# A fused attention and feed-forward kernel: AV and the second feed-forward on two 64-row halves from the third batch on

## The chip, the cores and the metric

One Trainium2 chip; the program runs on 1 of its cores. The metric is device time in microseconds, the median of the runs. The core's engines are TensorE (PE in the profile, and PEld for its weight loads), VectorE (DVE), ScalarE (ACT), GpSimd (POOL) and SyncE (SP, which here only issues DMAs). Matmuls write to PSUM, which has eight banks of 512 f32 a partition.

## The reference, cut to what matters

Attention with 16 query heads on 4 key/value heads over 8 batches of 384 positions, then a feed-forward with a squared relu over all 3072 rows:

```python
k = np.repeat(k, group, axis=1); v = np.repeat(v, group, axis=1)    # group = 4
scores = (1 / np.sqrt(64)) * np.matmul(q, k.transpose(0, 1, 3, 2))
attn = np.exp(scores - np.max(scores, axis=-1, keepdims=True))
attn = attn / (np.sum(attn, axis=-1, keepdims=True) + 1e-09)
attn_out = np.matmul(attn, v)                         # (8, 16, 384, 64)
x = attn_out.transpose(0, 2, 1, 3).reshape(3072, 1024)
h = np.maximum(x @ w_in, 0.0)                         # w_in 1024 x 2048
out = h * h @ w_out                                   # w_out 2048 x 1024
```

Inputs and output are f32; the kernel computes in bf16 with f32 sums. It leaves out the subtraction of the maximum, and gets the sum of a softmax row from a column of ones that is appended to v.

## The kernel before, in words

**A recorder with a clock.** The kernel is not written as loops for each engine. A class `Recorder` takes operations one by one (`R.add`, line 45): the engine, a function that issues the instructions, the tiles read and written, and a cost in us. It derives what each operation must wait for, keeps an estimated clock for each engine, and at the end `emit` (line 86) writes each engine's instructions in the order of recording, with semaphore waits. The operations are chosen by the loop at line 694: at each step it lists the candidates (scores `sc`, AV `av` and `av2`, a piece of the feed-forward `ffn`, some transposes) with the time at which each could start by the estimated clocks, and takes the one of best rank among those that are ready. `R.when` gives such a time; `used` and `pick` (line 200) choose a PSUM bank.

**The work of one batch.** A batch has 384 rows, three tiles of 128.

- Scores (`burst_small`, matmuls at line 362): kT times qT for each head. The head size is 64, so a matmul uses 64 of the 128 rows of the array, and two run side by side, one on rows 0 to 63 and one on rows 64 to 127, in two banks. ACT takes both banks at once through exp into `expT` (line 372).
- AV (`av`, matmuls at line 388): eight chunks a batch, each 18 matmuls with all 128 rows: the stationary operand is a 128 x 128 block of expT, the moving one 65 columns of `v_aug`. A chunk goes to one bank, in two parts of nine; between the two the loop can't put anything else (`av2` is ranked 2 and always ready). DVE then takes the reciprocal of the sums (line 397) and multiplies (line 403) into `o_sb`; after each second chunk SP transposes two chunks by DMA into `xT` (line 408).
- The first feed-forward: 16 tiles of 128 columns of w_in, each a sum over 8 blocks of 128 rows. In most batches this runs as quads of four tiles on 64-row halves (`quad`, matmuls at line 483): a pair of half matmuls works on two tiles at a time, in two banks, and a second phase swaps the halves, so that each bank gets both halves of the sum. The second phase waits for the first (`after`), since two halves must not write one bank at the same time; the phases of two pairs take turns. The banks are 4 to 7. A quad's eight pieces have eight half matmuls of 384 columns each. DVE takes the relu (line 496) and most of the squares (line 503), ACT a few squares (line 500), into `h2T`. Scores of the next batch are put between these pieces (`split` is true in this stretch). The last batch and part of the first use `up_part` instead (line 446), with 128 rows.
- The second feed-forward (`downs`, `down_part`, matmuls at line 545): for each of two column halves and three row tiles, 16 matmuls of 128 rows x 512 columns in four parts of four, alternating between banks 6 and 7. DVE copies the bank to `y_sb` (line 554) and SP stores it (line 557).

**The order.** In the steady state, the loop for feed-forward batch b first records the quads of b with the scores of b + 1 between their pieces, then seven AV chunks of b + 1, one part of the second feed-forward, the last AV chunk, and the rest of the second feed-forward of b. So scores and quads use 64-row halves, AV and the second feed-forward all 128 rows. SP's queue then holds four xT transposes, the kT and qT transposes for a later batch, and the six output stores. POOL's queue holds the loads of q, k and v, which wait for those transposes, and a copy into v_aug (line 275).

Of the kernel before, what the change touches and what calls it, by code (L numbers as in the profile page):

```python
# [5 lines left out]
ALU = mybir.AluOpType  # L6
# [135 lines left out]
def bass_gqa_attention__then__ffn_squared_relu_kernel(  # L142
# [12 lines left out]
    HKV = 4  # L155
# [249 lines left out]

    def turn_o_dma(b, g):
        o = (b * HKV + g) % NO
        R.add("sync", lambda e: e.dma_start_transpose(
            out=xT[b % NXT][:, 2 * g:2 * g + 2, :].rearrange("p c (i t) -> p (c i) t", i=NJ),
            in_=o_sb[o].ap().rearrange("p s f d -> p (s f d)")),  # L410
            reads=[("o_sb", o, 0), ("o_sb", o, 1)], writes=[("xT", b % NXT, 2 * g), ("xT", b % NXT, 2 * g + 1)],
            dma=f"turn_o{o}", cost=0.9, shared=(7.0, 1.1))
# [99 lines left out]
    def up_tile(b, c):  # L512
        at = []
        return [up_part(b, c, at, k0, k0 + 4) for k0 in (0, 4)]

    def downs(b):

        items = []
        for jj in range(2 if b == 0 else 0):
            ats = [[] for _ in range(NJ)]  # L520
            for tiles in ((0, 1), (2,)):
                for half in range(2):
                    for i3 in tiles:
                        for part in (2 * half, 2 * half + 1):
                            items.append(down_part(b, jj, i3, 512 * jj, 512 * jj + 512, part, ats[i3]))
        for jj in range(2 if b else 0):
            for i3 in range(NJ):
                last = b == B - 1 and (jj, i3) == (1, NJ - 1)
                for c0, c1 in ((512, 896), (896, 1024)) if last else ((512 * jj, 512 * jj + 512),):
                    at = []  # L530
                    for part in range(4):
                        items.append(down_part(b, jj, i3, c0, c1, part, at))
        return items

    def down_part(b, jj, i3, c0, c1, part, at):
        n = c1 - c0

        def piece():
# [11 lines left out]
            if part == 3:  # L550
                yb = y_n[0] % (2 * NY)
                y_n[0] += 1
                ysl = y_sb[yb // 2][:, (yb % 2) * 512:(yb % 2) * 512 + n]
                R.add("vector", lambda e: e.tensor_copy(ysl, bank(i)[:, 0:n]),  # L554
                      reads=[("bank", i)], writes=[("y", yb)], cost=0.08 + n / 960)
                rows = out[b * S:(b + 1) * S, :].rearrange("(p j) f -> j p f", j=NJ)[i3]
                put = lambda: R.add("sync", lambda e: e.dma_start(rows[:, c0:c1], ysl),
                                    reads=[("y", yb)], writes=[("out", b, i3, c0)], dma=f"y{yb}", cost=0.6)
                stored.append(("out", b, i3, c0))
                if b:  # L560
                    put()
                else:
                    held_back.append(put)

        need = [("w_out", jj, part // 2)] + [("h2T", c) for c in range(4 * part, 4 * part + 4)]
        return 0, need, (6, 7) if part == 0 else None, piece

# [62 lines left out]
    LOW, MID, HIGH = tuple(range(6)), (4, 5), (6, 7)  # L630
    smalls = []
# [60 lines left out]
    av_open = None  # L692
    margin = 0.5
    while av_q or av_open or sc_q or o_q or lanes or ff["now"] or ff["tiles"] or ff["down"]:
# [35 lines left out]
        if av_open is not None:  # L730
            cand.append((now, 2, "av2"))
        elif av_q:
            b, c = av_q[0]
            needs = {(b, c // 2 * NJ + j, 3 * (c % 2) + t) for j in range(NJ) for t in range(3)}
            if needs <= scored and ff["b"] >= b - NXT + (not ff["tiles"]):
                cand.append((max(R.when(reads=av_reads(b, c)), open_bank(spare)) + wait, 2, "av"))
        if o_q:
            cand.append((max(R.when(reads=o_q[0][2]), open_bank(spare)) + wait, 3, "o"))
        at_edge = not ff["now"] and not lanes and av_open is None
        if sc_q:  # L740
# [4 lines left out]
            ok = ok and pairs // 2 * NJ + NEX > b * NU + max(x for _, x, _ in tiles)  # L745
            if b and not split:
                ok = ok and at_edge and (u > 0 or pairs >= 8 * b and ff["b"] == b - 1 and len(ff["tiles"]) >= 4)
# [19 lines left out]
        if f_head is not None:  # L767
            chunks, need, banks, piece = f_head
            if x_done[ff["b"]] >= chunks:
                t = R.when(reads=need)  # L770
                if banks:
                    t = max(t, max(open_bank([i]) for i in banks) if split or opening else open_bank(banks))
                cand.append((t, 5, "ffn"))
        if split and at_edge and len(ff["tiles"]) < 4 and not (sc_q and sc_q[0][1]):
            split = False
            R.clock["tensor"] += 0.1
            continue
        if split:
            inside = [x for x in cand if x[2] in ("sc", "ffn")]
# [7 lines left out]
        ready = [x for x in cand if x[0] <= now + (0.0 if split else 0.05)]  # L787
        what = min(ready, key=lambda x: x[1]) if ready else min(cand)
# [3 lines left out]
        if split and what[2] not in ("sc", "ffn"):  # L792
            split = False
# [9 lines left out]
        elif what[2] == "av":  # L803
            b, c = av_q.pop(0)
            av_open = (b, c, av(b, c, spare))
            next(av_open[2])
        elif what[2] == "av2":
            b, c, rest = av_open
            av_open = None
# [11 lines left out]
        elif what[2] == "sc":  # L821
            b, u = sc_q.pop(0)
            if b and not split:
                split = True
                R.clock["tensor"] += 0.1
# [5 lines left out]
        else:  # L831
            if opening:
                split = True
                R.clock["tensor"] += 0.1
# [31 lines left out]
```

## Time and profile before

| what | value |
|---|---|
| median of 3 runs | 418.99 us (418.98 to 420.0) |
| profiled execution, its span | 417.1 us; its own time is not listed apart, so the runs' median stands beside it, 1.9 us longer |
| granted TensorE clock | 1.000 |
| PE matmuls / weight loads | 4322 / 4322 |
| L545, second feed-forward | 168.2 us busy, x784 |
| L483, quads | 160.0 us busy, x1728 halves |
| L362, scores | 53.9 us busy, x384 halves |
| L388, AV | 39.0 us busy, x1152 |
| L397 and L403, DVE after AV | 186 and 557 ns each, x64 |
| L496 and L503, relu and square on DVE | 552 and 568 ns each |
| L554, copy of the result on DVE | 691 ns for 512 columns |

The span is the time from the first to the last instruction of the program on the core; the runs' time is a little longer, since it has the launch's edges too. "Busy" counts the time in which at least one instruction of a group runs. Matmuls overlap: a matmul of 384 columns shows 323 ns of its own, but the next can start long before it ends, so the pace is read from the starts. The chain of work that ended last is followed back from the last instruction to what released it; its rows in order of time give the start, the time to the next row, the engine and line, and the number of instructions. A timeline row gives the start, the length, the engine and line, the shapes (rows*columns of the array, then the moving operand) and how many instructions were merged. Times are from the start of the span. In PEld rows a bracket gives idle time of the loading unit and what the profile thinks ended it.

### The profile page before, as it was taken

How to read it: one execution, taken by the hardware profiler on the slowest of the kernel's cores; microseconds unless marked ns; L12 is line 12 of the kernel's file. 1: busy time of each engine (PE TensorE's matmuls, PEld its weight loads, DVE VectorE, ACT ScalarE, POOL GpSimd, SP SyncE). 2: the span in 40 equal slices, each digit the busy share in tenths (PEclk: the TensorE clock that was granted, in tenths of full speed). 3: DMA queues.
4: the chain of work that ended last, by engine and by line, in shares of the span. 5: the costliest groups of instructions: out<-in, count | busy, mean ns of one | idle time of the engine just before them, and what ended most of it. 6: DMA issues, size and time to landing. Idle time of an engine off the chain costs nothing.

```text
span 417.1 us, 9610 instructions
## 1 busy us (share of the span) xinstructions
PE 413.2 (99%) x4322; PEld 235.2 (56%) x4322; DVE 202.1 (48%) x438; ACT 158.7 (38%) x180; POOL 47.4 (11%) x62
## 2 busy tenths in 40 slices
PE   8999999999999999999999999999999999999997
PEld 6565754557445564455645565455744557446544
DVE  3765751487314682156712666135842458324312
ACT  6958510386018510384005830069000970004300
POOL 8580000323003000200030000000000000000000
PEclk9999999999999999999999999999999999999999
DMA  9999999999989029900599006710052001420012
GB/s 181 188 190 194 206 186 176 234 182 128 191 152 160 7 52 194 203 10 2 75 214 168 2 2 108 184 52 2 3 126 77 27 2 21 127 78 5 0 75 77
DMA packets 96921, 44.40 MB, mean 106 GB/s; under 512 B 77296, under 2 KB 90864, under 8 KB 96880
## 3 DMA queue, kind: packets, MB, share of 16 engines
q0 software_dynamic: 36544, 17.44, 32.7%
q1 hardware_dynamic: 59664, 25.86, 28.4%
q8 instruction: 34, 0.56, 0.6%
q10 hardware_dynamic: 672, 0.49, 0.4%
q14 instruction: 7, 0.06, 0.0%
HBM read 35.65 MB, written 12.58 MB: 116 GB/s over the span
## 4 chain that ended last, share of the span: by engine, by line
PE 97%; ACT 2%; DVE 0%; issue 0%
PE ps L545 40%; PE ps L483 34%; PE ps L388 8%; PE ps L362 8%; PE ps L446 6%; ACT expT L372 2%; PE ps L608 1%; PE ps L421 0%; PE ps L336 0%; PE ps L316 0%; PE ps L299 0%; DVE y_sb L554 0%
## 5 line engine op out<-in xcount | busy, mean ns | idle before, releaser
L372 ACT ACTIVATE expT<-ps 128x1024 bf16<-128x1024 f32 (+1 forms) x145 | 135.9, 1033 | 132.6 <-PE ps L362 132.6
L545 PE MATMUL ps<-w_out_sb,h2T 128*128 128x512 bf16 (+2 forms) x784 | 168.2, 375 | 0.0
L483 PE MATMUL ps<-xT,w_in_sb 64*128 64x384 bf16 x1728 | 160.0, 323 | 0.0
L545 PEld LDWEIGHTS ps<-w_out_sb,h2T 128*128 128x128 bf16 x784 | 75.1, 98 | 86.6
L483 PEld LDWEIGHTS ps<-xT,w_in_sb 64*128 64x128 bf16 x1728 | 83.0, 94 | 57.8 <-DVE hr L496 2.5
L496 DVE TENSOR_SCALAR hr<-ps 128x384 f32<-128x384 f32 x108 | 55.2, 552 | 76.8 <-PE ps L483 76.8
L554 DVE COPY y_sb<-ps 128x512 f32<-128x512 f32 (+2 forms) x49 | 33.3, 680 | 112.1 <-PE ps L545 112.1
L362 PE MATMUL ps<-qT,kT 64*128 64x256 bf16 (+2 forms) x384 | 53.9, 324 | 0.7 <-ACT expT L372 0.6
L503 DVE TENSOR_TENSOR h2T<-hr 128x384 bf16<-128x384 f32 x102 | 51.8, 568 | 0.0
L388 PEld LDWEIGHTS ps<-v_aug,expT 128*128 128x128 bf16 x1152 | 36.9, 97 | 5.5 <-ACT h2T L500 1.3
L388 PE MATMUL ps<-v_aug,expT 128*128 128x65 bf16 x1152 | 39.0, 193 | 0.0
L403 DVE TENSOR_TENSOR o_sb<-ps,rinv 128x384 bf16<-128x384 f32 x64 | 35.7, 557 | 2.2
L446 PE MATMUL ps<-xT,w_in_sb 128*128 128x384 bf16 x160 | 27.5, 326 | 0.0
L456 ACT ACTIVATE h2T<-hr 128x384 bf16<-128x384 f32 x20 | 10.3, 523 | 44.1 <-DVE hr L454 44.1
L362 PEld LDWEIGHTS ps<-qT,kT 64*128 64x128 bf16 x384 | 17.7, 94 | 15.8 <-issue 1.7
L275 POOL COPY v_aug<-v_st 128x768 bf16<-128x768 bf16 x8 | 7.0, 874 | 153.7 <-PE ps L388 91.1
L500 ACT ACTIVATE h2T<-hr 128x384 bf16<-128x384 f32 x6 | 3.1, 522 | 50.0 <-DVE hr L496 50.0
L446 PEld LDWEIGHTS ps<-xT,w_in_sb 128*128 128x128 bf16 x160 | 15.4, 98 | 10.0 <-issue 0.2
L454 DVE TENSOR_SCALAR hr<-ps 128x384 f32<-128x384 f32 x20 | 10.9, 556 | 11.8 <-PE ps L446 11.7
L241 POOL DMA_DIRECT2D q_st<-in_q_dram x17 | 14.9, 887 | 1.0 <-POOLq L851 0.8
L397 DVE RECIPROCAL rinv<-ps 128x6 f32<-128x6 f32 x64 | 11.9, 186 | 2.4 <-PE ps L388 2.4
L209 POOL DMA_DIRECT2D k_st<-in_k_dram x7 | 5.3, 756 | 48.4 <-DMA qT<-q_st 48.4
(32 smaller groups left out, 63.3 us busy)
## 6 DMA issues: line engine op xcount, KB each, us to landing
out_dram<-y_sb SPq DMA_DIRECT2D x47, 256.0 KB, 2.7
q_st<-in_q_dram POOLq DMA_DIRECT2D x14, 384.0 KB, 8.0
w_in_sb<-in_moe_w_in_dram POOLq DMA_DIRECT2D x8, 512.0 KB, 15.2
w_out_sb<-in_moe_w_out_dram POOLq DMA_DIRECT2D x4, 1024.0 KB, 29.2
v_st<-in_v_dram POOLq DMA_DIRECT2D x8, 192.0 KB, 10.0
k_st<-in_k_dram POOLq DMA_DIRECT2D x7, 192.0 KB, 5.3
q_st<-in_q_dram POOLq DMA_DIRECT2D x3, 192.0 KB, 5.2
xT<-o_sb SPq DMA_TRANSPOSE x28, 2.8
```

The lines of the kernel that those rows point to most:

```text
L241: i = R.add("gpsimd", lambda g: g.dma_start(q_st[st][:, h0:h1, :], q[b, h0:h1].rearrange("h (p j) d -> p h (j d)", j=NJ)), writes=[("q_st" ...
L362: mm = pe.matmul(ps[:, base + x, m * wide:(m + 1) * wide], kT[b % 2][64 * x:64 * x + 64, u, :], q_cols(b, u // NJ, x, c0, c0 + wide))
L372: R.add("scalar", lambda e: e.activation(dst, src, AF.Exp, scale=0.125), reads=keys, writes=[("expT", (b * NU + u) % NEX, t) for u, _, _ i ...
L388: m = pe.matmul(po[:, f - 6 * s2, 0:D + 1], w, v_aug[b % 2][:, g * NJ + j, 0:D + 1], start=(j == 0), stop=(j == NJ - 1))
L397: R.add("vector", lambda e: e.reciprocal(rinv[r].ap().unsqueeze(2), po[:, :, D:D + 1]), reads=[("bank", i)], writes=[("rinv", r)], cost=0.22)
L403: R.add("vector", lambda e: e.tensor_tensor(dst, srcv, rbv, ALU.mult), reads=[("bank", i), ("rinv", r)], writes=[("o_sb", o, s2)], cost=0.48)
L446: m = pe.matmul(bank(i)[:, 0:S], w_in_sb[:, kc, c * 128:(c + 1) * 128], xT[b % NXT][:, kc, :], start=(kc == 0), stop=(kc == NKC - 1))
L483: m = pe.matmul(bank(4 + xs[x])[:, 0:S], w_in_sb[r, kc, c * 128:(c + 1) * 128], xT[b % NXT][r, kc, :], start=(phase < 2 and kc == 0), stop ...
L496: R.add("vector", lambda e, r=r, i=i: e.tensor_scalar_max(hr[r][:, :], bank(4 + i)[:, 0:S], 0.0), reads=[("bank", 4 + i)], writes=[("hr", ...
L503: hr_read[r] = (R.add("vector", lambda e, c=c, r=r: e.tensor_tensor(h2T[:, c, :], hr[r][:, :], hr[r][:, :], ALU.mult), reads=[("hr", r)], ...
L545: m = pe.matmul(bank(i)[:, 0:n], h2T[:, c, i3 * 128:(i3 + 1) * 128], w_out_sb[:, c, c0:c1], start=(c == 0), stop=(c == NFC - 1))
L554: R.add("vector", lambda e: e.tensor_copy(ysl, bank(i)[:, 0:n]), reads=[("bank", i)], writes=[("y", yb)], cost=0.08 + n / 960)
```

## The change

For feed-forward batches 2 to 6 (`on_halves`), and AV of batches 3 to 7 that is recorded with them:

- AV runs on halves (`av_halves`). A chunk owns a pair of banks, (0, 1) or (2, 3) in turn. Its first part has nine pairs of half matmuls, each 64 rows x 65 columns: rows 0 to 63 go to the first bank and rows 64 to 127 to the second. The second part swaps the halves, and waits for the end of the first part's last matmul. DVE's reciprocal and multiplication read both banks at once, three blocks from each.
- Parts of AV are kept apart: `since` counts the pieces of feed-forward since the last AV part, and an AV part is taken only after one such piece, or after two among the quads. AV may begin among the last quads, once the scores of the next batch are all recorded.
- The second feed-forward runs on halves (`down_pair`): three pairs of tiles, in banks (4, 5), (6, 7) and (2, 3), each in two phases of four pieces of eight half matmuls x 512 columns; the second phase swaps the halves and waits for the first. The pieces of the pairs take turns. The copies of a pair's two banks and its two stores are recorded together, after its last piece.
- The tiles of the first feed-forward in the last batch may use banks 0 to 3 in place of 6 and 7.
- The recorder's estimate for entering or leaving the stretch of quads, 0.1 us, is 0 where both sides are on halves.

```diff
+    def on_halves(b):
+        return 2 <= b < B - 1
+
+    def av_halves(b, c, pairs):
+
+        g, s2 = c // 2, c % 2
+        p = pick_pair(pairs)
+        held.update(p)
+
+        def mm(pe, y):
+            for n in range(NJ):
+                for j in range(NJ):
+                    for x in range(2):
+                        f, h = 6 * s2 + NJ * x + n, (x + y) % 2
+                        r = slice(64 * h, 64 * h + 64)
+                        w = expT[r, (b * NU + g * NJ + j) % NEX, f % 2, (f // 2) * 128:(f // 2) * 128 + 128]
+                        m = pe.matmul(ps[:, p[x], n * DP:n * DP + D + 1], w, v_aug[b % 2][r, g * NJ + j, 0:D + 1],
+                                      start=(n + j + y == 0), stop=(n + j + y == 2 * NJ - 1))
+            return m
+
+        keys = [("bank", i) for i in p]
+        lead = R.add("tensor", lambda pe: mm(pe, 0), reads=av_reads(b, c), writes=keys, cost=0.285)
+        yield lead
+        held.difference_update(p)
+        R.add("tensor", lambda pe: mm(pe, 1), reads=av_reads(b, c), writes=keys, cost=0.285, after=(lead,))
...
@@ downs
+        if on_halves(b):
+            t = [(jj, i3) for jj in range(2) for i3 in range(NJ)]
+            p, q, r = [down_pair(b, t[2 * n:2 * n + 2], (4, 6, 2)[n]) for n in range(3)]
+            items = p[0:4] + q[0:2] + p[4:8] + q[2:4]
+            for n in range(4):
+                items += [r[n], q[4 + n]]
+            items += r[4:8]
-        for jj in range(2 if b else 0):
+        for jj in range(2 if b and not on_halves(b) else 0):
...
+    def down_pair(b, tiles, base):
...
+                def mm(pe):
+                    for c in range(4 * k, 4 * k + 4):
+                        for h in range(2):
+                            x, r = (y + h) % 2, slice(64 * h, 64 * h + 64)
+                            jj, i3 = tiles[x]
+                            m = pe.matmul(bank(base + x)[:, 0:512], h2T[r, c, i3 * 128:(i3 + 1) * 128],
+                                          w_out_sb[r, c, jj * 512:(jj + 1) * 512],
+                                          start=(y + c == 0), stop=(y == 1 and c == NFC - 1))
+                    return m
+
+                ends.append(R.add("tensor", mm, reads=need, writes=[("bank", base + x) for x in range(2)],
+                                  cost=4 * (512 / 2400 + 0.0025), after=(ends[3],) if y == 1 and k == 0 else ()))
+                if len(ends) == 8:
+                    held.difference_update((base, base + 1))
+                    for x, (jj, i3) in enumerate(tiles):
+                        store(b, i3, 512 * jj, 512 * jj + 512, base + x)
...
@@ the loop that chooses
+    since, AMONG = 9, 2
...
+            late = on_halves(ff["b"]) and not (sc_q and sc_q[0][0] == ff["b"] + 1)
+            inside = [x for x in cand if x[2] in ("sc", "ffn") or late and (x[2] == "av2" or x[2] == "av" and since >= AMONG)]
...
+        if since < (AMONG if split else 1) and on_halves(ff["b"]):
+            ready = [x for x in ready if x[2] not in ("av", "av2")] or [] if split else ([x for x in ready if x[2] not in ("av", "av2")] or ready)
...
+        since = 0 if what[2] in ("av", "av2") else since + (what[2] == "ffn")
```

In the instructions as recorded, a batch's loop now reads: scores and quads as before; in the last two quads an AV part after every second piece, four in all, and a fifth after the last; then eleven AV parts, each behind one piece of the second feed-forward; then the remaining 13 pieces of it with no AV between. `store` holds what `down_part` did for the copy and the store. On SP the order is three xT transposes, two stores, the fourth xT transpose, the kT and qT transposes, and the other four stores. TensorE has 5522 matmuls and as many weight loads in place of 4322.

## The prediction

> **What bounds the kernel now.** I read the page's busy shares first, then its chain of work that ended last:
>
> ```profile
> PE 413.2 (99%) x4322; PEld 235.2 (56%) x4322; DVE 202.1 (48%) x438; ACT 158.7 (38%) x180; POOL 47.4 (11%) x62
> PE 97%; ACT 2%; DVE 0%; issue 0%
> ```
>
> TensorE is never long without a matmul, and 97% of the chain is TensorE's own; the 2% of ACT lies in the first 13 us. So neither a transfer nor another engine holds the middle of the run, and the question is only at what pace the matmuls follow each other. The chain in order of time shows it for the end of one batch's loop and the start of the next (start us, us, what):
>
> ```profile
> 297.94 3.94 PE ps L388 x126
> 301.89 0.86 PE ps L545 x4
> 302.75 0.55 PE ps L388 x18
> 303.30 19.86 PE ps L545 x92
> 323.15 0.54 PE ps L362 x4
> 323.69 1.30 PE ps L483 x16
> ```
>
> Paces from it: the second feed-forward (L545) 19.86 / 92 = 0.216 us a matmul of 128 rows x 512 columns; the first on halves (L483) 1.30 / 16 = 0.081 us a half, so 0.1625 us a pair of 64-row halves x 384 columns; AV (L388) 0.55 / 18 = 0.0304 us a matmul of 128 x 65. The step from 384 to 512 columns is 0.0533 us for 128 columns, 0.416 ns a column, and leaves 2.5 ns a matmul over: a pair of halves costs the same as one full matmul of that width. 65 columns would be 29.6 ns by the same line. So everything runs at the column rate, and what is left over is small. The chain has it at two places: 126 AV matmuls at 0.0304 are 3.83, and 3.94 stand there; four score halves (L362, two pairs of 512) should be 0.43, and 0.54 stand there. Both are where TensorE goes from 64-row halves to 128 rows or back. The timeline puts a number on it (start us, us, engine and line; three windows):
>
> ```profile
> 322.13 1.03 PE L545 MATMUL ps<-w_out_sb,h2T 128*128 128x512 bf16 x4
> 323.09 0.60 PE L362 MATMUL ps<-qT,kT 64*128 64x512 bf16 x4
> ...
> 372.14 1.03 PE L545 MATMUL ps<-w_out_sb,h2T 128*128 128x512 bf16 x4
> 373.01 0.49 PE L446 MATMUL ps<-xT,w_in_sb 128*128 128x384 bf16 x2
> ...
> 347.15 0.81 PE L483 MATMUL ps<-xT,w_in_sb 64*128 64x384 bf16 x8
> 347.89 0.20 PE L388 MATMUL ps<-v_aug,expT 128*128 128x65 bf16 x1
> ```
>
> Four L545 matmuls are due 4 x 0.216 = 0.863 after their first starts. At 372.14 the next operation also has 128 rows, and it starts 0.87 later: on time. At 322.13 the next is on halves, and it starts 0.96 later. At 347.15 four pairs are due 0.65 later, at 347.80; AV starts at 347.89. The single records give 95 to 97 ns at all nine such places between 147.6 and 347.7 us. **One change of row mode costs 0.096 us**; I know of no other idle time in these batches.
>
> **The change, part by part.** *Removed:* the loop of feed-forward batch 2 starts at 122.7 us on halves in both kernels. From there to the end of batch 6 the old one changes mode nine times (AV of batches 3 to 7 begins at 147.6, 197.6, 247.6, 297.6 and 347.6; scores and quads resume at 172.7, 222.7, 272.8 and 322.8). The new one stays on halves, and changes once at the end, to L446, where the old one did not (373.01 above). Eight fewer: 8 x 0.096 = **-0.77 us**.
>
> *Second feed-forward on halves:* 5 batches x 96 matmuls become 480 pairs of 64 x 512. Score pairs of that shape stand in the old trace at the column rate (two in 0.43, as at 80.33 us in the chain), and L483 pairs show the same; so 0.216 a pair, no change. Three pairs of tiles each own two banks (4 and 5, 6 and 7, 2 and 3) and their turn-round is interleaved: a second phase, which adds to banks that the other half wrote, waits for the end of the first phase's fourth piece, with at least two pieces, 1.7 us, between. The last pair leaves two copies to VectorE at once. L554 copies take 0.69 us and, like the relus (0.55 long, 0.475 apart), should start some 0.08 less apart, 0.61 (an estimate); the second ends about 0.39 + 0.61 + 0.69 = 1.7 us after the last matmul starts (0.39 is that matmul's own length), and the scores that want banks 2 and 3 stand one matmul, one score pair and two quad pieces behind it, 0.216 + 0.216 + 1.30 = 1.73 us. That just fits; 0 to 0.05 us a batch, at most +0.25, and I take 0.
>
> *AV on halves:* 5 x 8 x 18 = 720 full matmuls become 720 pairs of 64 x 65, in parts of nine pairs. The old trace has no pair narrower than 256 columns, so this price is bounded. From below: the column rate, 29.6 ns a pair against 30.4 now: 720 x 0.8 = -0.6 us. From above: each half costs a full matmul's 30.4, so 60.8 a pair: +21.9 us. I take 30.4, no change, by the weight loads and the order of issue:
>
> ```profile
> 347.31 0.26 PEld L483 LDWEIGHTS ps<-xT,w_in_sb 64*128 64x128 bf16 x4
> 347.89 0.39 PEld L388 LDWEIGHTS ps<-v_aug,expT 128*128 128x128 bf16 x11 [0.32 <-ACT h2T L500]
> ```
>
> Four half loads are over 0.26 us after the first began, which is one pair's 0.1625 and one load of 0.094 (its mean in the groups by shape): two halves load side by side. Eleven full loads follow each other by 0.029. In the single records the second half starts 3 ns behind the first, matmul and load alike, four instructions in 5 ns. The sequencer's own waits (records that no view lists) show how far it runs ahead: it passed the wait for AV's v_aug at 346.03 us, 20 matmuls before AV's first at 347.89, and at 97.3 us it passed eight instructions within 48 ns of a semaphore. A part's 18 halves therefore stand ready when the wide piece ahead of it (0.65 us among quads, 0.86 in the second feed-forward) ends.
>
> A rule of the Trainium skill speaks against this: "TensorE: Matmul & The Clock Gate", section "Wait — 56ns, not 53.3ns?", says that starts of matmuls never come closer than about 25 ns, however narrow they are. By it a pair is 50 ns, and the sum would be 720 x 19.6 = +14.1 us, not 0; the 3 ns between two halves in this trace say that the rule does not hold between row halves, though none here is that narrow.
>
> *What moves with AV:* the old order is seven AV chunks (126 matmuls) in a block, then one more; the new one spreads 16 parts over the last quads and the first half of the second feed-forward. Each chunk's reciprocal (0.186) and multiplication (0.557) move with it. DVE is the engine to look at: after the last quad ends it owes two relus and three squares at 0.475 and 0.467 apart, 0.95 + 1.4, and a start of 0.2, 2.6 us, before the fourth piece of the second feed-forward, which reads the last four h2T tiles. Ahead of that piece stand three pieces of 0.863 and four AV parts of 0.274: 3.7 us. Cover of 1.1 us; one more chunk's 0.74 in front still fits. AV's second part waits for its first part's end with a whole piece between. Of TensorE's queue, all that follows waits behind such a wait, so these are the places where it would hurt. On SP the fourth xT transpose now stands behind two output stores, some 6 us later than before, and lands about 7 us ahead of the next batch's quads; kT and qT transposes behind it and the POOL loads that wait for qT serve a batch later. None of it is on the path.
>
> **Sum.** -0.77 + 0 + 0 + 0 = -0.77 us. The profiled span is 417.1 us, the median of the runs 418.99; the 1.9 us around the span are not touched. 418.99 - 0.77 = **418.2 us**, -0.18%.
>
> **Rivals.** A measurement of this kernel can tell about 0.3%, 1.26 us, from no change.
>
> *AV loses its last nanosecond too.* Old AV loses 0.8 ns a matmul against the column rate, with a 35 ns step after about every four of 29. If pairs drop that, -0.77 - 0.6 = -1.4 us, 417.6 us, just over the 0.3%. For it: nothing in wide pairs shows such a step. Against: the load of 128 columns is the same.
>
> *The narrow pairs are paced by instructions, not columns: slower.* Place: the 80 AV parts. Twice the instructions in the same 0.55 us a chunk; the mechanism decides from 30.4 + 0.77 / 720 = 31.5 ns a pair, where the gain is gone, and from 30.4 + (0.77 + 1.26) / 720 = 33.2 ns the change is slower by over 0.3%. Price if halves wait in turn: +21.9 - 0.8, 440.1 us; if a pair takes 35 ns, 720 x 4.6 - 0.77 = +2.5, 421.5 us. For it: no pair under 256 columns in the trace. Against: the 3 ns and the run-ahead.
>
> *A wait takes the place of the mode change.* The two places above with covers of 1.1 us (h2T) and about nothing (banks 2 and 3). If each batch stood 0.5 us, +2.5 - 0.77 = +1.7, 420.7 us. Against: only DVE work not seen in the old order could do it.
>
> *The 0.096 us is not the mode's and stays:* 419.0 us. Against: it appears at each change and is missing at L545 to L446 and L545 to L388.
>
> **Chances.** Forecast 0.45; AV's nanosecond gone 0.20; pairs of 33 to 45 ns 0.13; pairs of 45 to 61 ns 0.12; a wait 0.06; no effect 0.04. Faster by over 0.3%: 0.20. Within: 0.45 + 0.04 = 0.49. Slower: 0.13 + 0.12 + 0.06 = 0.31. The range goes from the second case less a tenth or two, 417.4, to the 35 ns pair, 421.5; outside are the 0.12 and the upper half of the 0.13.
>
> **What would show it.** Timeline at L545's successor: a quad or score on time, no 0.096. Chain: the batch period, 50.01 us now (the rows at 273.14 and 323.15), at 49.8. A part of 18 AV halves in 0.27 us; 0.54 means the instruction rival. Eight down halves in 0.86. Waits: TensorE behind DVE at the first scores or at the fourth down piece means the third rival. The forecast is wrong if a narrow pair takes over 33 ns.

## The result, and the profile after

| | median us | runs | |
|---|---|---|---|
| before | 419.08 | 12 (418.95 to 420.06) | |
| after | 418.24 | 12 (418.0 to 418.7) | ratio 0.9978, 95% interval 0.997 to 0.9987 |

The change saves 0.84 us, by the interval 0.5 to 1.3 us. The profiled execution of after took 418.54 us, its span 416.7 us at a granted clock of 1.000. The page's busy shares and its chain for the kernel after:

```profile
PE 413.1 (99%) x5522; PEld 236.3 (57%) x5522; DVE 202.9 (49%) x438; ACT 159.3 (38%) x180; POOL 46.8 (11%) x62
PE 97%; ACT 1%; DVE 1%; issue 0%
```

1200 more matmuls, and TensorE is as busy and as long in the chain as it was: a share of busy time can't show this change. It has to be read from starts. The chain of after in order of time (start us, us, what): the first quads of a batch, then from the first piece of its second feed-forward to the next batch:

```profile
223.39 1.30 PE ps L524 x16
...
249.29 0.86 PE ps L635 x8
250.43 0.86 PE ps L635 x8
251.57 0.86 PE ps L635 x8
...
261.80 11.22 PE ps L635 x104
273.24 1.30 PE ps L524 x16
```

Eight halves of 512 columns take 0.86, four pairs at 0.2158. Between two of them lies an AV part: 250.43 - 249.29 - 0.86 = 0.28 us for nine pairs of 65 columns. The 104 halves then run through to 273.02, and one pair of scores (L362, 0.21, too short for this list) leads to 273.24, where the next quads start. The chain's row for the same place a batch earlier starts at 223.39: a batch takes 49.85 us, where it took 50.01.

The timeline of TensorE shows the joints (start us, us, line and shape; three windows of after):

```profile
272.64 0.38 PE L635 MATMUL ps<-w_out_sb,h2T 64*128 64x512 bf16 x2
272.86 0.38 PE L362 MATMUL ps<-qT,kT 64*128 64x512 bf16 x2
273.07 1.46 PE L524 MATMUL ps<-xT,w_in_sb 64*128 64x384 bf16 x16
274.41 0.61 PE L362 MATMUL ps<-qT,kT 64*128 64x512 bf16 x6
...
370.81 1.89 PE L635 MATMUL ps<-w_out_sb,h2T 64*128 64x512 bf16 x16
372.63 0.66 PE L487 MATMUL ps<-xT,w_in_sb 128*128 128x384 bf16 x3
```

One pair of 512 columns from 272.64 leads to the scores at 272.86 and these to the quads at 273.07, each 0.216 later: the 0.096 us at the old scores is gone. The eight pairs from 273.07 are due 1.30 later, at 274.37, and the second scores start at 274.41, some 0.04 late (0.036 by the single records). At the end eight pairs from 370.81 are due 1.73 later, at 372.54; L487 with 128 rows starts at 372.63, late by the one change of mode that is left.

I went through all starts of the single records and took off what each matmul costs at the column rate (columns / 2.4 + 2.5 ns). From 123 to 373 us only six places of more than 25 ns remain in after: changes of mode at 123.04 and 372.32 (96 ns each), and the 0.036 us at 174.5, 224.4, 274.2 and 324.1. Between those two changes lie 249.28 us; in before the same stretch has 250.08. So -0.80 us there, +0.096 for the new change at its end: **-0.71 us**. Behind it both kernels take 44.06 us to the end of the span, so the other banks of the last batch play no part. The span differs by only 0.4 us because the first 123 us took 0.3 us longer in this execution. TensorE's sequence of matmuls there is the same in before, after and experiments 1 to 7, yet its length varies from 122.7 to 123.8 us in their profiles. The stretch is therefore the better measure, and the experiments are read by it too.

### The profile page after: what moved, and what is told of

It is laid out like the page before. It is cut to its first block, busy times and chain, and to the rows that moved or that the text cites. A ratio compares the mean times of both kernels' runs of the same rounds, so it can differ in the third digit from the quotient of the medians.

```text
span 416.7 us, 11990 instructions
## 1 busy us (share of the span) xinstructions
PE 413.1 (99%) x5522; PEld 236.3 (57%) x5522; DVE 202.9 (49%) x438; ACT 159.3 (38%) x180; POOL 46.8 (11%) x62
## 4 chain that ended last, share of the span: by engine, by line
PE 97%; ACT 1%; DVE 1%; issue 0%
PE ps L524 34%; PE ps L635 25%; PE ps L593 15%; PE ps L362 8%; PE ps L487 6%; PE ps L429 5%; PE ps L388 3%; ACT expT L372 1%; PE ps L693 1%; DVE hr L495 0%; PE ps L462 0%; DVE kT L325 0%; PE ps L336 0%; PE ps L299 0%; DVE qT L343 0%
## 5 line engine op out<-in xcount | busy, mean ns | idle before, releaser
L524 PE MATMUL ps<-xT,w_in_sb 64*128 64x384 bf16 x1728 | 163.3, 323 | 0.0
L635 PE MATMUL ps<-w_out_sb,h2T 64*128 64x512 bf16 x960 | 113.4, 376 | 0.0
L609 DVE COPY y_sb<-ps 128x512 f32<-128x512 f32 (+2 forms) x49 | 31.9, 677 | 89.2 <-PE ps L635 45.7
L635 PEld LDWEIGHTS ps<-w_out_sb,h2T 64*128 64x128 bf16 x960 | 42.6, 94 | 42.7
L593 PE MATMUL ps<-w_out_sb,h2T 128*128 128x512 bf16 (+2 forms) x304 | 63.0, 368 | 0.0
L362 PE MATMUL ps<-qT,kT 64*128 64x256 bf16 (+2 forms) x384 | 54.2, 326 | 0.5 <-ACT expT L372 0.4
L593 PEld LDWEIGHTS ps<-w_out_sb,h2T 128*128 128x128 bf16 x304 | 28.9, 98 | 32.3
L429 PEld LDWEIGHTS ps<-v_aug,expT 64*128 64x128 bf16 x1440 | 32.7, 94 | 16.3
L429 PE MATMUL ps<-v_aug,expT 64*128 64x65 bf16 x1440 | 34.9, 190 | 0.0
L487 PE MATMUL ps<-xT,w_in_sb 128*128 128x384 bf16 x160 | 27.5, 326 | 0.0
L362 PEld LDWEIGHTS ps<-qT,kT 64*128 64x128 bf16 x384 | 17.7, 94 | 15.3 <-ACT expT L372 1.5
L444 DVE TENSOR_TENSOR o_sb<-ps,rinv 128x384 bf16<-128x384 f32 x40 | 22.3, 557 | 1.4
L487 PEld LDWEIGHTS ps<-xT,w_in_sb 128*128 128x128 bf16 x160 | 15.4, 98 | 10.2 <-issue 0.6
L442 DVE RECIPROCAL rinv<-ps 128x6 f32<-128x6 f32 x40 | 7.7, 193 | 25.5 <-PE ps L429 24.9
```

The lines of the kernel that those rows point to most:

```text
L362: mm = pe.matmul(ps[:, base + x, m * wide:(m + 1) * wide], kT[b % 2][64 * x:64 * x + 64, u, :], q_cols(b, u // NJ, x, c0, c0 + wide))
L429: m = pe.matmul(ps[:, p[x], n * DP:n * DP + D + 1], w, v_aug[b % 2][r, g * NJ + j, 0:D + 1], start=(n + j + y == 0), stop=(n + j + y == 2 ...
L444: R.add("vector", lambda e: e.tensor_tensor(dst, po[:, :, :, 0:D], rv.to_broadcast([128, 2, NJ, D]), ALU.mult), reads=keys + [("rinv", r)] ...
L487: m = pe.matmul(bank(i)[:, 0:S], w_in_sb[:, kc, c * 128:(c + 1) * 128], xT[b % NXT][:, kc, :], start=(kc == 0), stop=(kc == NKC - 1))
L524: m = pe.matmul(bank(4 + xs[x])[:, 0:S], w_in_sb[r, kc, c * 128:(c + 1) * 128], xT[b % NXT][r, kc, :], start=(phase < 2 and kc == 0), stop ...
L593: m = pe.matmul(bank(i)[:, 0:n], h2T[:, c, i3 * 128:(i3 + 1) * 128], w_out_sb[:, c, c0:c1], start=(c == 0), stop=(c == NFC - 1))
```

## Experiments

My theory: a change of row mode costs 0.096 us, halves cost the column rate and nothing else, and the gain is the changes that are gone. The rivals: the gain is that AV is spread out; narrow halves do cost something that the spreading hides; the covers (banks, h2T) are what keeps it from being a loss.

**1. AV with 128 rows at the places of its halves.** Order, banks and waits stay as they are after.

```diff
-                    for x in range(2):
-                        f, h = 6 * s2 + NJ * x + n, (x + y) % 2
...
+                    f = 6 * s2 + NJ * y + n
+                    w = expT[:, (b * NU + g * NJ + j) % NEX, f % 2, (f // 2) * 128:(f // 2) * 128 + 128]
+                    m = pe.matmul(ps[:, p[y], n * DP:n * DP + D + 1], w, v_aug[b % 2][:, g * NJ + j, 0:D + 1],
+                                  start=(j == 0), stop=(j == NJ - 1))
```

> AV of batches 3 to 7 with all 128 rows again, nine matmuls a part, in exactly the places, banks and waits that the changed kernel gives its half parts. Mode theory (the time is the columns at their pace plus 0.096 us for each change of row mode, and halves cost nothing else): each of 80 parts now stands between wide halves, 160 more changes, +15.4 us over the changed kernel, and up to +2 more for the first narrow matmuls after each change, so 433.6 to 436. Order theory (the gain came from spreading AV over the last quads and the second feed-forward): the order is the same, 418.2. Instruction theory (narrow halves cost issue time that the wide pieces just hide): half the AV instructions, 418.2 or a little less.

Measured: 435.60 us, ratio 1.0404 (1.0386 to 1.0421). The chain of this kernel, with two pieces of quads and two pieces of the second feed-forward:

```profile
197.47 1.41 PE ps L522 x16
...
203.97 0.97 PE ps L633 x8
205.32 0.97 PE ps L633 x8
```

The same work takes 1.30 and 0.86 in after; each row is longer by the 0.1 us of the change that ends it, and 205.32 - 203.97 - 0.97 = 0.38 us stand for the AV part in place of 0.28: its own 0.28 and the change that ends it. In the records 160 changes more than in after cost 95 to 96 ns each, 15.3 us of the 17.4 that lie between the two kernels; the rest lies mostly in starts behind a change (AV loses 2.3 ns a matmul over the column rate instead of 0.9). So the price is the mode's, and the spread order without the halves would be a loss of 16.5 us. These items add up to the 17.0 us by which the stretch is longer than in after, so the order has no gain of its own.

**2. The second feed-forward on halves, AV as before.**

```diff
-        if av_q and len(av_open) < 1 + on_halves(av_q[0][0] - 1):
+        if av_q and len(av_open) < 1:
...
-            late = on_halves(ff["b"]) and not (sc_q and sc_q[0][0] == ff["b"] + 1)
+            late = False
...
-            rest = av_halves(b, c, places) if on_halves(b - 1) else av(b, c, spare)
+            rest = av(b, c, spare)
```

> One part alone: the second feed-forward of batches 2 to 6 on halves, AV with all 128 rows in one block of 144 between quads and second feed-forward. Mode theory: a change into AV and one out of it in each of five batches and one at the end, 11, where the changed kernel has 1 and the old one 9: 0.96 us over the changed kernel, 0.19 over the old one, 419.2 to 419.3. A theory that halves of 512 columns are themselves faster or slower by 2 ns a pair would move it by 480 x 2 ns, 1 us, to 418.3 or 420.2.

Measured: 433.5 us, ratio 1.0341 (1.0318 to 1.0364). A miss, and a useful one. The waits of TensorE in this kernel (us in total, times, longest):

```profile
PE ps L635 <- DVE o_sb L403: 8.9, 5, 3.4
```

Its timeline of TensorE at the worst of the five places:

```profile
255.82 1.09 PE L388 MATMUL ps<-v_aug,expT 128*128 128x65 bf16 x26
260.35 4.45 PE L635 MATMUL ps<-w_out_sb,h2T 64*128 64x512 bf16 x24 [3.44 <-DVE o_sb L403]
```

The first pair of tiles wants banks 4 and 5. The old AV block had used banks 0 to 5 in quick succession, and VectorE still owed one multiplication every 0.69 us for them. TensorE stands at that point in each batch, 8.9 us in all by the view, 9.7 by the starts (2.2, 0.8, 3.6, 2.2 and 0.8, each with the change of mode there). The loss is 14.4. The table by windows shows most of the rest (window; busy us and count of PE, PEld, DVE, ACT, POOL; granted clock; DMA):

```profile
257.40:260.81 3.41, 0.46 (x6) 0.23 (x8) 2.75 (x9) 0.00 (x0) 0.41 (x1) 1.00 0.79 154
260.30:263.80 3.50, 3.45 (x20) 1.31 (x22) 0.00 (x0) 0.00 (x0) 0.00 (x0) 0.57 0.83 159
260.81:264.22 3.41, 3.41 (x20) 1.24 (x18) 0.00 (x0) 0.00 (x0) 0.00 (x0) 0.50 0.82 158
264.00:268.00 4.00, 4.00 (x38) 1.78 (x36) 0.00 (x0) 0.00 (x0) 0.00 (x0) 0.97 1.32 174
```

After the stand of 3.6 us the granted clock is 0.57 on the mean of the next 3.5 us, and 0.50 from 260.81 to 264.22 us: 20 halves in that time, where 38 go into 4.0 us later. A pair takes 0.427 us there in place of 0.216. The same follows the second of the two stands of 2.2 us (0.50 from 315.42 to 318.83), and not the first, nor those of 0.8. Twice some eight pairs at 0.21 us more are 3.4 us; with the 9.7 that makes 13.1. "TensorE: Matmul & The Clock Gate", section "What's actually happening", in the Trainium skill, says that the clock falls to half after an idle window of about 3.4 us and needs as long a busy one to come back. The two stretches of 3.41 us at half clock agree with the second part. For the first, the trace shows that the window need not be idle throughout: the two stretches begin 54.61 us apart, 16 times 3.41, and in the 3.41 us before each, TensorE was busy for 0.46 and 1.36 us. The first stand of 2.2 us (153.5 to 155.7) lies across 155.0 us, a border of the same grid of 3.41 us, and in the two stretches beside that border TensorE was busy for 2.06 and 2.71 us. That the clock is judged on such a grid fits these cases; no run here tests it.

**3. The same, with the first pair in banks 6 and 7.**

```diff
-            p, q, r = [down_pair(b, t[2 * n:2 * n + 2], (4, 6, 2)[n]) for n in range(3)]
+            p, q, r = [down_pair(b, t[2 * n:2 * n + 2], (6, 4, 2)[n]) for n in range(3)]
```

> The second feed-forward alone on halves again, now with its first pair of tiles in banks 6 and 7 and the second in 4 and 5, so that it doesn't wait for the banks that VectorE is still reading for the last AV chunks. Theory now (modes, and the run of e2 lost 14 us to that wait): 11 changes of mode, 0.19 us over the old kernel, and in one batch of five the last AV chunks fall on banks 4 and 5 late enough for one stand of about 0.8 us: 419.9 to 420.1. Rival (AV in one block in front of halves is bad in itself, whatever the banks): 425 or more.

Measured: 420.82 us, ratio 1.0038 (1.0021 to 1.0056); the stretch takes 251.44 us. No long stand is left and no half clock, so the bank was the cause of the loss in 2. It is still 1.4 us longer than before, and here I had miscounted: the loop puts one piece of the second feed-forward between the last AV chunks, on halves now, so that each batch changes mode four times. Inside the stretch, without the change that opens it, that is 20 against 9 of before: 11 more at 0.095 are 1.04 us of the 1.36, the four places of 0.036 another 0.14, and the rest lies in the starts of AV (0.06) and of the second feed-forward (0.12). The price of a change holds; half of the change alone loses, since it makes more joints than it takes away.

**4. AV parts not kept apart.**

```diff
-        if since < (AMONG if split else 1) and on_halves(ff["b"]):
+        if False:
...
-            inside = [x for x in cand if x[2] in ("sc", "ffn") or late and (x[2] == "av2" or x[2] == "av" and since >= AMONG)]
+            inside = [x for x in cand if x[2] in ("sc", "ffn") or late and (x[2] == "av2" or x[2] == "av")]
```

> The changed kernel with the rule of spacing taken away: up to 72 narrow halves follow each other (runs of 72, 36 and 18 in a batch). Mode theory: still 30.4 ns a pair, and a first part's end is covered by the first part of the next chunk, 418.2, within 0.4 us; at most a few tenths from lead-to-second-part waits. Instruction theory: beyond the 18 halves that stand ready the pairs fall to two matmuls' pace, 63 pairs a batch x 30 ns x 5 = +9.6 us, 427.8.

Measured: 418.5 us, ratio 0.9987 (0.9978 to 0.9995); the stretch takes 249.33 us. Its timeline, two AV parts in a row among the quads:

```profile
197.97 0.71 PE L429 MATMUL ps<-v_aug,expT 64*128 64x65 bf16 x36
198.51 0.81 PE L524 MATMUL ps<-xT,w_in_sb 64*128 64x384 bf16 x8
```

18 pairs in 0.54 us; by the single records these and the longest runs, of 36 pairs, keep the same 30.5 ns a pair. Wide pieces between the parts are not needed for the pace from the third batch on.

**5. AV begun after the quads only.**

```diff
-            late = on_halves(ff["b"]) and not (sc_q and sc_q[0][0] == ff["b"] + 1)
+            late = False
```

> The changed kernel, but AV is begun only after the last quad, not among the last quads; the last two chunks then follow each other without wide pieces between. Mode theory: the same changes, the same columns, 418.2 within 0.3. Order theory: beginning AV among the quads is what gains, so back to 419.1.

Measured: 422.5 us, ratio 1.0083 (1.0069 to 1.0097), a miss. TensorE's waits in this kernel:

```profile
PE ps L635 <- DVE o_sb L444: 3.1, 5, 0.6
```

Its timeline of all engines at the first of the five:

```profile
161.41 1.25 PE L429 MATMUL ps<-v_aug,expT 64*128 64x65 bf16 x72
...
162.67 0.56 DVE L444 TENSOR_TENSOR o_sb<-ps,rinv 128x384 bf16<-128x384 f32 x1
...
163.28 1.62 PEld L635 LDWEIGHTS ps<-w_out_sb,h2T 64*128 64x128 bf16 x18 [0.74 <-DVE o_sb L444]
163.28 1.90 PE L635 MATMUL ps<-w_out_sb,h2T 64*128 64x512 bf16 x16 [0.62 <-DVE o_sb L444]
```

AV now ends later, against the third pair of tiles, whose banks 2 and 3 hold AV's last chunk but one: VectorE's multiplication for it must end (162.67 + 0.56) before L635 goes on at 163.28. In after, the same multiplication ends about 2.1 us before the third pair starts, by the timeline and the order of pieces. By the starts 0.78 us stand in each of five batches, 3.9 us.

**6. The same, with the third pair begun two pieces later.**

```diff
-            items = p[0:4] + q[0:2] + p[4:8] + q[2:4]
-            for n in range(4):
-                items += [r[n], q[4 + n]]
-            items += r[4:8]
+            items = p[0:4] + q[0:4] + p[4:8] + q[4:6] + [r[0], q[6], r[1], r[2], r[3], q[7]] + r[4:8]
```

> AV begun only after the last quad, as in e4, but the third pair of tiles (banks 2 and 3) starts two pieces of the second feed-forward later. Bank theory (e4's 0.78 us a batch is the third pair's wait for VectorE to leave banks 2 and 3): the wait is gone, and the time is the changed kernel's, 418.2 within 0.3. Order theory (beginning AV among the last quads gains by itself): 419 or more still, and up to e4's 422.5.

Measured: 418.58 us, ratio 0.9988 (0.9973 to 1.0004); the stretch takes 249.285 us, after's 249.278. The stands are gone. Beginning AV among the quads gains nothing of its own; it keeps AV and the third pair apart in two banks, and another order of pieces does that as well.

**7. No turns between the pairs of tiles.**

```diff
-            items = p[0:4] + q[0:2] + p[4:8] + q[2:4]
...
+            items = p + q + r
```

> The pieces of the second feed-forward's pairs in plain order, first phase then second, pair after pair. In the first pair an AV part still stands between the phases; in the second and third nothing does, so the second phase's first matmul waits for the end of the matmul just before it: 0.376 us of its own length and some 0.02 for the semaphore, where the next is due after 0.216. Cover theory: 0.18 us x 2 x 5 batches = +1.8 us, 420.0, and the waits stand at exactly these ten places. Rival (TensorE orders the two phases by itself and the wait costs nothing): 418.2.

Measured: 420.84 us, ratio 1.0037 (1.0022 to 1.0052). Ten stands, at the second phases of the second and third pair in each of five batches, of 229 ns each where I expected 180: 2.3 us, of the 2.6 that it lies above after. The next start comes 0.445 us after the last one of the phase, which is that matmul's own 0.376 us and some 0.07 from its end to the next start, where I had expected 0.02.

**8. Halves from the second batch on, its AV not kept apart.** With the order of pieces of 6.

```diff
-        return 2 <= b < B - 1
+        return 1 <= b < B - 1
...
-        if since < (AMONG if split else 1) and on_halves(ff["b"]):
+        if since < (AMONG if split else 1) and on_halves(ff["b"]) and ff["b"] > 1:
```

> A try at a better version: halves from the loop of feed-forward batch 1 on (AV of batch 2), with the third pair started two pieces later and no spacing of AV parts in that first batch, where AV comes late. Mode theory: two changes fewer, -0.19 us: 418.05, if no wait takes their place; the profile has 5 changes fewer than 0.096 each would need to be seen only in the trace, since the difference is below what the runs tell. Against: AV of batch 2 runs in series of 72 halves late in the second feed-forward, and its transposes land nearer to the next quads.

Measured: 421.26 us, ratio 1.0045 (1.0026 to 1.0063), 3.2 us above the 418.05 expected. TensorE's timeline in AV of this batch:

```profile
107.00 0.53 PE L429 MATMUL ps<-v_aug,expT 64*128 64x65 bf16 x24
109.56 0.35 PE L429 MATMUL ps<-v_aug,expT 64*128 64x65 bf16 x12 [2.03 <-issue]
109.75 1.03 PE L632 MATMUL ps<-w_out_sb,h2T 64*128 64x512 bf16 x8
110.62 0.71 PE L429 MATMUL ps<-v_aug,expT 64*128 64x65 bf16 x36
111.17 1.02 PE L632 MATMUL ps<-w_out_sb,h2T 64*128 64x512 bf16 x8
112.03 0.71 PE L429 MATMUL ps<-v_aug,expT 64*128 64x65 bf16 x36
112.58 1.03 PE L632 MATMUL ps<-w_out_sb,h2T 64*128 64x512 bf16 x8
113.44 0.44 PE L429 MATMUL ps<-v_aug,expT 64*128 64x65 bf16 x18
113.72 0.38 PE L632 MATMUL ps<-w_out_sb,h2T 64*128 64x512 bf16 x2
114.94 2.33 PE L632 MATMUL ps<-w_out_sb,h2T 64*128 64x512 bf16 x20 [0.84 <-issue]
```

Two stands in the middle of a part and of a piece, 2.2 us and 1.0 us beyond the matmul before, where no semaphore is due ("issue": waiting for nothing that the profile shows). Count the matmuls from the first stand to the second: 12 + 8 + 36 + 8 + 36 + 8 + 18 + 2 = 128, with as many weight loads 256 instructions. The DMA records have packets of 16,384 bytes on the queue that the page calls instruction, and their number follows TensorE's instructions: 34 in before (2 x 4322 / 256 = 33.8), 37 in experiment 1 (37.5), 43 in after (43.1), 45 here (45.0). That fits instructions that come in blocks of 256, with TensorE standing at the border of a block twice in a row; the two stands are the 3.2 us. Two such packets began in this stretch, at 106.8 and 112.6 us, and took 1.1 and 1.05 us; a load of q was under way until 111, one of v until 112.6. A block of AV halves alone is used up in 64 pairs x 30.5 ns = 1.95 us. That the fetch falls behind is argued from these numbers together; what passes between the packet's end and the going on, 1.6 and 1.3 us, the trace does not show.

**9. The same from the second batch on, AV kept apart as after.**

```diff
-        return 2 <= b < B - 1
+        return 1 <= b < B - 1
```

> Halves from feed-forward batch 1 on, as in e6, but with the changed kernel's spacing of AV parts and its order of pairs. In e6 TensorE stood 2.2 and 1.0 us amid narrow halves while the trace shows it waiting for nothing; each time a 16 KB instruction fetch landed 1.3 to 1.6 us before it went on, and q loads kept the DMA engines busy. Fetch theory: runs of 36 to 72 narrow halves use up 88 instructions in 1.4 us, spaced parts some 52 in 1.14 us, so the fetches keep up and no stand without a named wait is over 0.3 us there; the time is 418.24 - 0.19 plus the two or three short waits for banks and first parts, up to 1.1 us: 418.2 to 419.3. Rival (something else in batch 1's AV, such as v_aug or the transposes): stands of 1 us and more stay, 420 or more.

Measured: 420.37 us, ratio 1.0028 (1.0019 to 1.0037). No stand of 1 us or more in AV of this batch; in its place there are five of 226 to 267 ns between 113.2 and 115.9, where parts follow each other and the second part or a bank is waited for, 1.3 us with one of 74 ns. The profiled run (421.46) is also the slowest of this kernel: 0.95 us of it stand at 67.1 us for the load of w_out, and 0.76 at 36.8 us for that of w_in. The stands at the blocks' borders are gone, as the theory of 8 has it; the time is not in its range of 418.2 to 419.3, and the profile explains that in part only, by those two loads. But what took them away is not settled: in those 3.2 us 126 halves follow each other after all, slowed by the waits, and the loads of q and v had landed by 107.8 and 109.4 us, where in 8 they ran until 111 and 112.6. Spacing, waits and load are not told apart. To begin at the second batch is no better either way.

**10. AV with 33 columns in place of 65, parts not kept apart.** The kernel leaves out half of v's columns, so it no longer computes the reference; it tells what paces a narrow pair.

```diff
-                        m = pe.matmul(ps[:, p[x], n * DP:n * DP + D + 1], w, v_aug[b % 2][r, g * NJ + j, 0:D + 1],
+                        m = pe.matmul(ps[:, p[x], n * DP + 32:n * DP + D + 1], w, v_aug[b % 2][r, g * NJ + j, 32:D + 1],
...
```

> What sets AV's pace of 30.4 ns. Half of v's columns are left out of AV on halves (33 columns instead of 65, the sums kept), and in the AV with 128 rows two of three matmuls have 33 columns too; AV parts not kept apart. Column theory: 33 x 0.416 + 2.5 = 16.2 ns a pair. Weight-load theory (a 128-column load takes 30.4 ns, both halves side by side): 30.4 stays for pairs and for full matmuls alike. A floor for each matmul of about 25 ns: 50 ns a pair, 25 a full matmul.

Measured: 415.42 us, span 413.6, in a single run. Its timeline:

```profile
199.56 0.61 PE L430 MATMUL ps<-v_aug,expT 64*128 64x33 bf16 x36
200.01 1.02 PE L636 MATMUL ps<-w_out_sb,h2T 64*128 64x512 bf16 x8
```

18 pairs in 0.45 us are 25 ns a pair; the column rate would be 16.2. In the same kernel 128-row matmuls of 33 columns (AV of the first three batches) follow each other by 26.6 ns on the mean of the single records. So at 33 columns there is a floor of 25 to 27 ns, and it is the floor of a pair: two halves share it. Each half brings its own load of 128 columns of weights, so the runs do not tell whether the matmuls or the loads set it. The section "Wait — 56ns, not 53.3ns?" of "TensorE: Matmul & The Clock Gate", which the prediction weighed, has this floor at about 25 ns between starts; for single matmuls the number agrees, and for two halves the measurement decides against 50 ns a pair. At 65 columns AV, with 30.5 ns, stands 4 to 5 ns above the floor.

**11. The copy out of PSUM put at 0.13 us in place of 0.08 in the loop's estimates.** The loop then records a third piece of quads ahead of the scores that want banks 2 and 3.

```diff
-               reads=[("bank", i)], writes=[("y", yb)], cost=0.08 + n / 960)
+               reads=[("bank", i)], writes=[("y", yb)], cost=0.13 + n / 960)
```

> The changed kernel with the estimate of VectorE's copy raised by 0.05 us, which puts one more quad piece ahead of the score pair that wants banks 2 and 3 at the start of each batch. Theory: the stand of 36 ns there (four times in the changed kernel, none named in the forecast's sum) is the third pair's second copy, so it goes, -0.14 us; in time 418.1, not to be told from 418.24. Rival (the score pair itself is late for another reason, such as its kT): 36 ns stay.

Measured: 418.39 us, ratio 0.9984 (0.9975 to 0.9993). The chain of this kernel where after has 16 halves from 273.24:

```profile
273.24 1.95 PE ps L524 x24
```

All four stands of 0.036 us are gone, and from 123 to 373 us only the two changes of mode remain; the stretch takes 249.08 us, 0.20 less than after. A later start would also hide a late kT, so this run alone does not name the copy. The timeline of after does:

```profile
273.06 1.29 DVE L609 COPY y_sb<-ps 128x512 f32<-128x512 f32 x2 [2.16 <-PE ps L635]
274.40 0.33 PEld L362 LDWEIGHTS ps<-qT,kT 64*128 64x128 bf16 x6 [0.26 <-DVE y_sb L609]
```

The second copy ends at 273.06 + 1.29 = 274.35, and the scores start at 274.41; at all four places the records have 0.056 to 0.057 us between the two. In the runs' times experiment 11 can't be told from after, and no kernel here is measurably better than the changed one.

## Why the prediction was right, step by step

Forecast 418.2 us, measured 418.24, and within 0.3% of before, as the likeliest case had it. That the two agree to 0.04 us is luck: the interval of the saving is 0.8 us wide, and the median of before alone went from 418.99 with three runs to 419.08 with twelve.

- **Eight fewer changes of mode, -0.77 us: right.** The runs say -0.84, the stretch -0.71: eight changes at 0.0957 are -0.77, the fourth point's loss is +0.14, and smaller starts make up -0.09, 0.05 of it in AV, which the sum did not have. Experiment 1 prices 160 changes at 95 to 96 ns each, and experiment 3 shows the sign turning when changes are added.
- **AV halves at 30.4 ns a pair, no change: right.** 30.5 in after, 0.9 ns over the column rate, where 128-row AV lost 1.0. The rival that AV loses its last nanosecond fails: the loss stays. The rival of 35 or 60.8 ns fails by the same number, and experiment 10 shows why there was room: the floor is 25 to 27 ns and belongs to the pair. That there was so little room, 4 to 5 ns, I had not known; the 3 ns between two halves say nothing of how closely pairs can follow, so here the argument was luckier than it was good.
- **Second feed-forward on halves, no change: right.** 0.86 us for each piece of eight.
- **Banks 2 and 3, 0 to 0.05 us a batch, 0 taken: a small miss.** 0.036 us in each of four batches, 0.14 in all, inside the bound of 0.25 and at the place named, the scores behind two quad pieces. The estimate of the copy was right: it ends 1.71 us after the last matmul starts (1.7 estimated), 0.02 before the scores are due at 1.73. What the sum had at nothing is the time from the copy's end to TensorE's start, 0.056 us; 0.056 - 0.02 are the 0.036. Experiment 11 removes them.
- **h2T's cover of 1.1 us: held.** In the single records the last square ends 1.00 us ahead of the fourth piece in each of the five batches.
- **Second phases with at least two pieces, 1.7 us, between: misread, without harm.** That is so for the first pair of tiles. In the diff's order the second pair has only r[0] between q[3] and q[4], and the third only q[7] between r[3] and r[4]: one piece, which leaves 0.70 us from the end of the first phase to the start of the second. It suffices: 7 shows some 0.07 needed there.
- **A wait takes the place of the mode change: it did not, beyond the 0.14.** But three such places cost time in the experiments. Two of them, the waits for AV's multiplications ahead of the first and the third pair of tiles (experiments 2 and 5: 8.9 us and then half clock, 3.9 us), the prediction does not name, and the expectations of 2 and 5 left them out as well. The third, the turns between phases, it names as a cover (experiment 7: 2.3 us).
- **0.096 not the mode's: refuted** by experiment 1.

## What to carry to other kernels

Look for changes between 64-row halves and full rows, and count the joints at 0.096 us each: pairs of halves run at the pace of full matmuls, so putting the whole steady state in one mode was a gain here, and a part of it a loss. What the mode costs is small beside what one bank in the wrong place costs, so for each moved operation follow the bank to its last reader and price the stand. Judge a change of this size by a stretch of the trace between two equal instructions, since here the start of the run alone varied by 1.2 us between profiles, more than the change is worth.

## What the runs showed of the hardware that I had not expected

- TensorE was granted half its clock for 3.41 us after it had stood for 3.6 us (experiment 2), and after one of two stands of 2.2 us; in the 3.41 us before, it had been busy for 0.46 and 1.36 us.
- The 16 KB packets on the instruction queue (0.9 to 1.5 us each) are as many as blocks of 256 of TensorE's instructions, and it stood 2.2 and 1.0 us at two places 256 instructions apart while q and v were loaded or just after (experiment 8). In the third and later batches the same narrow parts ran without a stand.
- Two row halves of 33 columns share one floor of 25 to 27 ns between starts (experiment 10).
- With the kernel's wait between the phases and nothing else to do, a matmul that adds to a bank which the other half has just written starts 0.445 us after the last start, 229 ns late at 512 columns (experiment 7). From VectorE's last read of a bank to TensorE's next start in it pass 0.05 to 0.06 us (after, experiments 2 and 5).
